# A gated residual in one VectorE pass, row means added back by ScalarE, and an order written out as a list

## The chip, the cores and the metric

The kernel runs on one core of a Trainium2 chip. A core has five engines that run their own instruction streams side by side: TensorE (PE in the profile, its weight loads PEld), VectorE (DVE), ScalarE (ACT), GpSimd (POOL) and SyncE (SP), whose stream here is little else than DMA issues. The metric is the device time of one launch in microseconds, smaller is better. Of the kernel before, three runs are shown: 843.17, 844.55 and 843.1 us, median 843.17.

## What is computed

The reference runs four sub-layers on a sequence of S = 2048 rows of D = 640 (all f32):

```
x = q
x = x + layernorm(x) * y            # A: gate
x = x + relu(layernorm(x) @ w1) @ w2  # B: MLP, Dff = 1728
x = x + layernorm(x) * y            # A again, same y
x = x + relu(layernorm(x) @ w1) @ w2  # B again, same weights
```

Here y is a long causal convolution (by FFT, over the sequence, for each channel) of kv = shortconv(k) * v with ssm_k, plus kv * ssm_D. It does not depend on x, so it is needed once. layernorm has no weights: (x − mean) / sqrt(var + eps) over a row of 640.

The fact that the change uses: layernorm does not see a constant added to a whole row. With r = 1/std and m the row mean, x + r(x − m)y = (x − m)(1 + r y) + m. If m is left out, the row that goes on differs from the reference's by a constant, which neither the next layernorm nor the matmuls behind it see. The constants have to be added back before the result is stored.

## The kernel before

**Tiling.** The 2048 rows are eight chunks of 256, each two row tiles of 128 x 640 (s = 0, 1). The convolution is done as matrix products on transposed data: `transform` turns kv and the filter into a short spectrum (tiles `pg`, `pt`, `pr`, with constant matrices `cG`, `cX`, `cM`), `products` multiplies spectra on VectorE (`pacc`, `pd`, `u`) and transforms back (`pq`, `qs`, then `yd` or `ys`). The finished y goes to a DRAM buffer `Y` and comes back by DMA as tile `y`, except for chunk 0 (the "direct" chunk), where `yd` is used straight from SBUF, and the last column blocks of some chunks, which are taken from `ys`.

**The MLP.** `prep` (L1115) does the gate and the second layernorm of one piece of a chunk, splits the result into two f16 parts (`xh`: high and low), transposes it to `xT`; `mm1` forms h as three f16 products of high and low parts (lines L1350, L1351, L1353; L1338 and L1340 for chunk 0), ScalarE and VectorE turn it into f16 `hh`, `hl` (L1493, L1494), `mm2` multiplies by w2 (L1322, L1323, L1325; tiles `o`, `oc`), and VectorE adds the scaled result to x (L1431). For the last chunks a scheme with fewer products is used (`wmm`, L1268). The weights are loaded as `ws` and scaled into f16 (`w`, L977).

**The gate.** `stats` (L1065) computes negm = −mean (ACT), the sum of squares (ACT, L1071), r (small ACT and DVE steps) and nmr = −r·mean, and then `xnA` = r·x + nmr on ACT (L1093). VectorE multiplies `xnA` by y (L1136, L1139 for the part from `ys`, L906 for chunk 0) and adds it to x with the row sum as a by-product for the next layernorm (L1143, L907 for chunk 0). Each is one instruction per row tile of 640 columns (chunk 0: pieces of 256, 256 and 128).

**Head and tail.** Before the first data arrive, PE runs matmuls on an identity that nobody reads (`spin`, L1602, and L1619 between the first real matmuls). VectorE adds `dDs` (ssm_D) to the first row of the filter tile `hf` (L538), and the matmuls `pg` of that tile follow. At the end the last pieces of `o` are added to x and stored (L1560, L1564, L1566; whole rows by L1437).

**What sets the order.** The program does not emit instructions directly: each step is handed to `Plan.op` with its engine, an assumed cost and the tiles that it reads and writes. A planner (`best`, `order`) then plays an event-driven schedule over these costs, with a rank for each step out of a table of numbers (`RANKS`), and emits the instructions of all engines in the resulting order. On the chip each engine runs its own stream in that order and waits on semaphores.

Of the kernel before, what the change touches and what calls it, by code (L numbers as in the profile page):

```python
# [22 lines left out]
P = 128  # L23
# [36 lines left out]
RANKS = (  # L60
    "D*!A2000311ONp91^@>D2mlEH3IGcL3;+!P4ge1T5C9PX5&#nb6aW<f762Cj7yuan8UPyr8~_~v9snNzAOIl%A^;-*BmgA<CIBY@C;$ThF90zBDF7`1E&wV3GypOHH2^jMIsiTZIRHHXK>$MlQUFu{"
    "Hvl^TLI6MjMgU*{R{&%HXaH;gZUA%uM*v6wNdQU!O8`s&O#n^+PXJH=SO8f7S^!%BTmW4FUI1SJJOF9{Q2==WeE@?1hX9iRqyUrvrU0t|umH9Iy8y!gFaS6JKLBq4MF3L(RsdoEWdLUYX#i~iaR7J#"
    "egJX+cL09?d;o#~ivWfIj{uecn*f~vq5ygTfB=O6i2#ZKkN}qepa7`=u>iRMp#Yo!W&s=l#Q@6y&j8Z^L;zI)VE}{xa{zS!hyaZMl>nLmp8$>kkpP$gr2wh`v;epOzW~Gl#{kIy%>btWtN^nBy#Txb"
    "zyQVo%mCH^+5qDK>HrV{E&)0L-vHzQ@BsAy^8k$jw*WH$B>^}AK>=9-VgXYDTLFs!YXOr1mI18+)dAZ9?f~=vN&#8{b^!$e3;`GcApwv9*8%7O>;d=z{Q>>~0s;pD+yM;&(E!x|*8toA-2mbM=m6^g"
    "@c{Aw_yBSNhXED=2mw_AkpcDq`T+d^0s#U5V*srHW&p1MYXGtUZ~(Ocb^y8ndjP=zfdI+?i~!OAk^tENnE>Dbo&e<lqX5tVr~udit^nQu?Evop`2hO>0RaR72LTTOz5wO`!T{+2$N>BR&H(-Z)Bpnk"
    "+W-;);Q$l?=Kvo8>;NYL_W&sY{{Sli3IQzv4goU(6#+Q`KmkYrPyto}TmfJKVF6_U009O82>}ZM4FMAY7XcmtZvh<vBLO4<ECCq-F#$9IHvu~VLIFkrOab!&O#xB?5dj(j8v!B#AOR);DgiP9F9AFO"
    "J^@7mO94><P61Z|WC3acXaQ^iZUJ)vh5>K^cL9O{dI5g{egT64hyjiPi~*7Xl>wRonE{>wp8=-<qXDS_ssXbBuK~FMxB<HXyaB=i!vV<w#{td(%>mN^(E;HBzyZVo<pKBtFab3IHUT{WL;*<wKLJAl"
    "SOHxDZ2@rsPXSZ`Ujb(UiUE%SV*zOabOC$;paG=;lmVy#t^uL}qyf4Cz5%fTv;npOtO2qC#sSa)$N|d%!2!hq$^py))B)cC;sNpj`~d+11p;*ecmaC>eF204i2;BCg#nxap#hfxn*q-O(gD~3<N>t-"
    "00P+o?E&=x`T-RJAOh(D69O0l`2h?9E&?+GECMtFKmr^BCjv17JOV}nNdiLxO#)K_TLMu6R{~!GWCC*ndIEj|umJ`F3IY)V83G*wA_6J`G6FUNI08KaK>|bqN&-#-R02{0S^{zcd;)(0ivo@Ulmd7H"
    "g#wKNk^+|kn*x;roC2f*s{*P5u>zq2rvj`3#R9eh!~($r%>vc}$O6>@&;rx~-vZ+T<^tLR-~#Fb1q1T}_X6nx?gI4!`~ndJ8v`E$CIdqQO9M{>w*i0xf&z#Fj{=hdnF6Q+uL8INxdOcczyiYp$pX&;"  # L70
    "*8<Z5+ybisy#ZbUfdRh(-2vVK-~rYF+5ztY?g8-u_5t((_W}O_0|E{L76JqU2?7rS3jz`X8Uh~zB?2S@D*`tHI|4oeNCI90EdpW!M*-&nc>(GHodFO6rU5kqMFLC$Y64IKSORVWbOM9|fdYpD`vC|7"
# [12 lines left out]
    "9|a}_F9kIPIt5MzS_N$dV+C*pN(7YzZv?gk&;-r|`vm<2vjn09w*<Qc!UV(w%>>{C<pk~oRRwPaSp{<idIf|9j0Keiodu!=hy|wwt_8RS#s$3v%>~j0)CJ20_66hwKn3&!Mg;=}3I#F+I0ZWeR|Rwh"
    "L<LI)dj(wuUIl&yg9U#DnFWCbrUkGCxdqAv&;`2%zy;3*+y&zW=mqNq>;(k|eFd5Y{sj&O7zQT>5(X0n83r5%9|j@@E(S6NHU>NfKn6_)Q3g{6Sq5JQU<P6aX9j8pZ3b}$a0Yb-c?Nw3e+GaC$OX;?"
    "(FN57+6CPO*#+JO<OSyi^9B3`<^}Hs0R{&K1O^HQ`2`jR9tI-@AO<D|5C$y<HwHBZItDQYK?XwxMg~;|M+Qy?TLxwZXa;TuRt8)Kb_RR~at3<_fd+&Ihz5)XiUyJfng*T*p$3lzmIjyxoCco;rUsn`"
    "qz0`9vj)8e!3M4dwg$=u+6L4H*apT1&IaHH?*``v@CM-q_67h4`343D{00RF3I`kqAO{Tx9S0-_D+ehDEe93{BL^=BF$XgTJqJbyNe4^^PX|s1QU_HBSqEGPI|g0`qXwl0s0OPBx(2)k#0JO)$p+O1"
    "%Lds7+XmbQ;|A&m0tW;K2nP%Y4hItl6bCQ|5(gUx83!^4IR{Y(R0miGUI%CgS_fhWZ3l1%cn5z6atDP6iwBVhp$Di3iU*Phtp~FQum`yZnFqZG#s|L##RtR(;|IwH%m>W}$_LU1=?Cox=LhZw*$3SR"
    "^9TF~{RadH2M8qyDhMtJJqSk#O9(&+L<mL*%?8s3U<Y9bX9sTwc?Wz4h6jlUj0cbhjt7$mng^Q)p9i7`rw6JBt_QaVwFkfly9dVyxCguk)(6f9$pr8OB?XuTwFSZj*9F@J^91Mw0tFHU7zG{$A_Xc1"
    "J_SPs>ILux_XYX|00ssI3<ePf7X}&z9R?}}F9taVJqA7oLIy|%Oa?y&YzBt~(*@rJjs@5Sp#{VR;sv|~?FHZk^#%9^<puo(@df_{0|p5O`vnaK6b2gxAqFJ|L<Ud>C<ZVFO9og5WCnN!g9e2Liv}YF"  # L90
    "E(Hh%6$U8=BnD3gQU*x{qy?%4tp&aX!3D<!%mv{E@&$7ScLsU}h6a%amj<8)u?DyXxdy5RuLipY-3ILj<_7f!{RROC)&?I30tQJ2S_TUSMFtNBD+XZ(GX`r0N(N~Leg<U*kOp)HjRuqkq6UHnn+B-{"
    "w+6ok#Rl;P{szYe(FXGd0|yBQ5eFp)9tS4}#RcvKjs}?qtOm3O%m&W}^aU&iGzK^ZR0dZDT?TIki3YF+7Y88+8V4c=E(bLSHwQZhKL<hwJO@DsMF(pKZU=D(bq9I}eFt3!l?Rgs-Uj6cl?K-arv}0X"
    ">ju6C^akGs`UVFF=>`i2_y!LL7zZW?{{|=rEC)0PItN1sbO(C}N(W5`cL#(Aj|Y|qqX(V`rUzpNhX(8hHU~!sKnG?AY6rCjvIf8g!v@d>(gxxN=mzoz_Xd;)oClZ(r3b4Au?MyXz6Zev$Oq5|*9Y7O"
    "@CWq=_Xqn200;vJ<p&-J5C>!jYzGwwUk54&J_mCLI0t?QX$OG^hX-~Cmj{9epa-c3uLp<+tOvRW%LmT~(+Bwn0SMIx-Ut2%1qciX6bKmz8VDQ+<Oc2rjR&#^!w13#-v{9b`vyb@NC!&?PzO^7R|i`M"
    "V+Vi-4+s?q5(pRwAqXc3F9<aVIS4xlEC@3QK?q3*RtQcAVF+djX9%4K<Ok>nqzCT@v<KP;^as%g{|D>`1_%lW_6H3J0tgWZ8wel>2?!$yDF`wMHwZ%rUI=OkN(fO1WC(Bwfe4HUk_eFql?Yb|X$V{h"
# [108 lines left out]
class Plan:  # L204
# [39 lines left out]
    def best(self):  # L244
        ranks = np.frombuffer(base64.b85decode(RANKS), "<u2").tolist()
        for o, r in zip(self.ops, ranks, strict=True):
            if o.prio[0] != CRIT:
                o.prio = (r, o.seq)
# [1499 lines left out]
```

## Time and profile before

| | |
|---|---|
| median of the runs shown | 843.17 us (843.1 to 844.55, 3 runs) |
| profiled execution, span | 841.6 us |
| PE busy | 833.6 us, 99% |
| DVE busy | 786.8 us, 93% |
| ACT busy | 522.8 us, 62% |
| DMA | 181.69 MB, mean 216 GB/s |
| chain that ended last | PE 79%, DVE 12%, DMA 3%, ACT 3%, issue 2% |

The profile is of one execution, whose span is from the first to the last instruction; the time of a run is taken on the device around it, and the runs shown lie 1.5 to 3.0 us above this span. A row such as `134.48 0.22 PE L1350 MATMUL h<-xT,w 128*128 128x128 f16 x1 [0.62 <-DVE hh L1494]` reads: start in us, duration in us, engine, line, operation, output and inputs, tile shape, count; in brackets how long the engine had been idle just before, and whose end it waited for. Durations overlap on PE, since the next matmul starts while the last one drains; how fast PE issues is read from the distance between starts. In a group's row, the numbers behind the bar are busy time in us, mean ns of one, and idle time ahead.

### The profile page before, as it was taken

The page shows a single profiled execution, that of the slowest core. Times are in us where ns is not written, and L with a number is a line of the kernel's source. Part 1 is how long each engine was busy: PE and PEld are TensorE (multiplying, and loading weights), DVE is VectorE, ACT ScalarE, POOL GpSimd, SP SyncE. Part 2 cuts the span into 40 slices and gives each one's busy share as a digit, 9 for nine tenths or more (in the row PEclk, how much of TensorE's full clock was granted, in tenths as well). Part 3 has the DMA queues.
Part 4 walks back from the last instruction along what each step waited for, and adds up shares of the span by engine and source line. Part 5 has one row for each costly group of instructions (what it writes and reads, how often), then busy time and mean ns, then how long its engine had stood idle before and what let it go on. Part 6 is the DMA issues. An engine that isn't in the chain of part 4 may idle for free.

```text
span 841.6 us, 20268 instructions
## 1 busy us (share of the span) xinstructions
PE 833.6 (99%) x8031; PEld 669.3 (80%) x8031; DVE 786.8 (93%) x1431; ACT 522.8 (62%) x1237; POOL 45.5 (5%) x56
## 2 busy tenths in 40 slices
PE   8999999999999999999999999999999999999998
PEld 7987887888888778777787777777777788888887
DVE  6999999999999999999999999999988799998775
ACT  5798887347776586647438574655524487868432
POOL 0000000000002111011110201010000000000000
PEclk9999999999999999999999999999999999999999
DMA  8995877987999997988998967688987466250400
GB/s 300 395 355 170 259 211 226 309 307 257 266 249 266 327 252 212 239 248 221 235 267 238 244 218 182 159 209 256 255 271 268 110 202 141 79 104 2 58 33 33
DMA packets 138145, 181.69 MB, mean 216 GB/s; under 512 B 53825, under 2 KB 95681, under 8 KB 138050
## 3 DMA queue, kind: packets, MB, share of 16 engines
q1 hardware_dynamic: 129586, 169.81, 67.4%
q0 software_dynamic: 8320, 10.49, 7.9%
q8 instruction: 63, 1.03, 0.5%
q14 instruction: 32, 0.26, 0.1%
q10 hardware_dynamic: 144, 0.10, 0.0%
HBM read 124.59 MB, written 34.08 MB: 189 GB/s over the span
## 4 chain that ended last, share of the span: by engine, by line
PE 79%; DVE 12%; DMA 3%; ACT 3%; issue 2%; SPq 0%; DVEq 0%; ACTq 0%
PE o L1268 10%; PE h L1350 8%; PE h L1351 8%; PE h L1353 8%; PE o L1323 7%; PE o L1322 7%; PE o L1325 6%; PE h L1338 4%; PE h L1383 2%; PE hs L1383 2%; PE h L1340 2%; PE oc L1322 2%; PE oc L1323 2%; PE oc L1325 2%; DVE pd L803 2%
## 5 line engine op out<-in xcount | busy, mean ns | idle before, releaser
L1350 PE MATMUL h<-xT,w 128*128 128x256 f16 (+1 forms) x1000 | 229.4, 249 | 0.9 <-DVE hh L1494 0.9
L1353 PE MATMUL h<-xT,w 128*128 128x256 f16 (+1 forms) x1000 | 229.2, 249 | 0.0
L1351 PE MATMUL h<-xT,w 128*128 128x256 f16 (+1 forms) x1000 | 229.2, 249 | 0.0
L1322 PE MATMUL o<-w,hh 128*128 128x512 f16 x336 | 127.3, 379 | 0.0
L1323 PE MATMUL o<-w,hh 128*128 128x512 f16 x336 | 127.3, 379 | 0.0
L808 DVE TENSOR_TENSOR pacc<-pacc,pd 128x1536 f32<-128x1536 f32 (+1 forms) x75 | 123.2, 1642 | 0.5
L1351 PEld LDWEIGHTS <-w 128*128 128x128 f16 x1100 | 107.6, 98 | 16.0 <-issue 1.8
L1350 PEld LDWEIGHTS <-w 128*128 128x128 f16 x1100 | 107.6, 98 | 14.5
L1353 PEld LDWEIGHTS <-w 128*128 128x128 f16 x1000 | 97.8, 98 | 6.3
L1493 ACT ACTIVATE hh<-h 128x512 f16<-128x512 f32 (+1 forms) x97 | 46.9, 485 | 69.1 <-PE h L1353 29.3
L1322 PEld LDWEIGHTS <-hh 128*128 128x128 f16 x672 | 65.7, 98 | 26.5
L1323 PEld LDWEIGHTS <-hh 128*128 128x128 f16 x672 | 65.8, 98 | 25.9
L803 DVE TENSOR_TENSOR pd<-Ax,Gx 128x768 f32<-128x768 f32 x83 | 78.3, 950 | 4.4 <-DMA Gx<-G 4.1
L1325 PE MATMUL o<-w,hl 128*128 128x512 f16 x208 | 78.8, 379 | 0.0
L1322 PE MATMUL oc<-w,hh 128*128 128x128 f16 x336 | 73.8, 220 | 0.0
L1323 PE MATMUL oc<-w,hh 128*128 128x128 f16 x336 | 73.6, 219 | 0.0
L532 ACT ACTIVATE tp<-kt,shs 128x256 f32<-128x256 f32 (+1 forms) x78 | 44.0, 577 | 26.8 <-DVE acc L606 20.8
L1325 PEld LDWEIGHTS <-hl 128*128 128x128 f16 x416 | 40.7, 98 | 24.5
L1338 PE MATMUL h<-xT,w 128*128 128x256 f16 (+1 forms) x400 | 57.9, 251 | 0.0
L1325 PE MATMUL oc<-w,hl 128*128 128x128 f16 x208 | 45.6, 219 | 0.0
L803 DVE TENSOR_TENSOR pd<-at,Gx 128x768 f32<-128x768 f32 x46 | 43.0, 950 | 0.7 <-DMA Gx<-G 0.5
L1338 PEld LDWEIGHTS <-w 128*128 128x128 f16 x400 | 35.9, 98 | 5.1
(284 smaller groups left out, 2010.3 us busy)
## 6 DMA issues: line engine op xcount, KB each, us to landing
Ax<-A SPq DMA_DIRECT2D x89, 384.0 KB, 4.2
Gx<-G SPq DMA_DIRECT2D x89, 384.0 KB, 4.4
A<-at SPq DMA_DIRECT2D x14, 768.0 KB, 6.3
G<-gt SPq DMA_DIRECT2D x14, 768.0 KB, 5.3
ws<-in_w SPq DMA_DIRECT2D x28, 320.0 KB, 6.8
y<-Y SPq DMA_DIRECT2D x22, 320.0 KB, 3.8
x<-in_q SPq DMA_DIRECT2D x16, 320.0 KB, 4.9
gs<-in_hF SPq DMA_DIRECT2D x20, 256.0 KB, 4.4
```

What stands on the lines that cost most here:

```text
L532: ACT.activation(o[:, i : i + m], kview(i, m, j), AF.Copy, scale=shs[:, t, j : j + 1])
L803: ew(f"mac{j % POOLMOD}", 768, lambda e, x=dst[i], av=av, gv=gv: e.tensor_mul(x.t, av(), gv()), [ax, gx], [dst[i]], pr_)
L808: dve(768 * (hi - lo), lambda lo=lo, hi=hi, pd=pd: DVE.tensor_add(acc[:, lo:hi], acc[:, lo:hi], pd[:, lo:hi]), [*sums[lo:hi], *dst[lo:hi]] ...
L1268: PE.matmul(b[:, c : c + w], x, y[:, z : z + w], start=done[i] == 1, stop=end, skip_group_check=fin)
L1322: PE.matmul(z, hh[:, c], wh[:, d], start=(j == JS[0] and i == 0 and (h == 0 or s == S[0])), stop=False)
L1323: PE.matmul(z, hh[:, c], wl[:, d], start=False, stop=end and tail)
L1325: PE.matmul(z, hl[:, c], wh[:, d], start=False, stop=end)
L1338: PE.matmul(p[:, z], wh, xv(t, x), start=b and x == 0, stop=e and x == 1)
L1350: PE.matmul(p[:, z], wh, xv(t, 0), start=b, stop=False)
L1351: PE.matmul(p[:, z], wh, xv(t, 1), start=False, stop=tail and e)
L1353: PE.matmul(p[:, z], wl, xv(t, 0), start=False, stop=e)
L1493: act(2 * R, lambda pv_=pv_, hh=hh: ACT.activation(hh.t, pv_(), AF.Relu), [src], [hh], URGENT)
```

## The change

**The gate.** `stats` for a gate no longer makes `nmr` and `xnA`; it returns r and negm. ACT makes t = r·y + 1 (two instructions where y comes in two parts), and VectorE does x = (x + negm)·t with the row sum in one instruction. So 44 multiplies leave VectorE's stream, and the 32 big `xnA` instructions of ACT become 44 for `t`. The row mean left out is kept: ACT writes it to `means` in the first gate, adds that of the second to it, and adds the sum to the row tile of x after the statistics of the second MLP (16 instructions of 128 x 640, L1109).

```diff
-            (0.19 * len(S), [r, negm], [nmr], lambda: [A(nmr[:, c], ...) for c in cols]),
+        if gated is not None:
+            a, layer = gated
+            if layer == 0:
...
+                act(2, lambda: ACT.activation(m[:, q_], negm[:, q_], AF.Copy, scale=-1.0), [negm], [m], FILL, 0.1)
+            else:
+                act(0, lambda: [ACT.activation(m[:, s : s + 1], negm[:, s : s + 1], AF.Identity, scale=-1.0, bias=m[:, s : s + 1]) for s in S], [negm, m], [m], FILL, 0.19 * len(S))
+            return r, negm
...
# prep, one row tile s
-            xns = stats(xs, sums, "A" + nm, S)
+            r, negm = stats(xs, sums, "A" + nm, S, gated=(a, layer))
-                ew("ay", cut, lambda e, s=s, xn=xns[s]: e.tensor_mul(xn[:, 0:cut], ys[s][:, 0:cut], xn[:, 0:cut]), ...)
+                gate_ = lambda o, i, s=s: ACT.activation(o, i, AF.Identity, scale=r[:, s : s + 1], bias=one.t)
+                act(cut, lambda s=s, t=t, gate_=gate_: gate_(t[:, 0:cut], ys[s][:, 0:cut]), [ys[s], r, one], [t], URGENT, 0.18)
-                dve(D, lambda ...: DVE.scalar_tensor_tensor(xs[s].t, xn.t, 1.0, xs[s].t, op0=ALU.mult, op1=ALU.add, accum_out=sums2[:, s : s + 1]), ...)
+                dve(D, lambda ...: DVE.scalar_tensor_tensor(xs[s].t, xs[s].t, negm[:, s : s + 1], t.t, op0=ALU.add, op1=ALU.mult, accum_out=sums2[:, s : s + 1]), ...)
...
+        for s in S if layer else ():
+            act(D, lambda s=s: ACT.activation(xs[s].t, xs[s].t, AF.Identity, bias=MEAN[a][:, s : s + 1]), [xs[s], MEAN[a]], [xs[s]], LATER, 0.1)
```

Chunk 0 gets the same two instructions for each of its pieces (L829, L830). A branch that sent the add through GpSimd and that no chunk took is dropped. In the weight norms, a matrix of ones becomes bf16 and four small matmuls read the upper half of their f32 operand.

**The order.** The planner and its ranks are gone; a table `ORDER` lists all steps in the order in which they are emitted:

```diff
-    def best(self):
-        ranks = np.frombuffer(base64.b85decode(RANKS), "<u2").tolist()
...
-        return self.order()
+    def table(self):
+        return [self.ops[k] for k in np.frombuffer(base64.b85decode(ORDER), "<u2")]
```

So the streams of all engines differ throughout, not at the gate alone. The start of SP's stream, which issues the first loads; before:

```order
L445 DMA cG<-in_cG 128x512
L515 DMA kt_0_157<-in_kT 128x262
L518 DMA hf_0_163<-in_hF 128x2x256
L439 DMA shs<-in_shk 128x20
L441 DMA dDs<-in_dD 1x640
L515 DMA kt_0_157<-in_kT 128x262
L518 DMA vt_0_186<-in_vT 128x2x256
L445 DMA cX<-in_cG 128x384
L518 DMA kt_2_202<-in_kT 128x2x262
L445 DMA cM<-in_cM 128x768
```

and after:

```order
L367 DMA cX<-in_cG 128x384
L440 DMA hf_0_176<-in_hF 128x2x256
L361 DMA shs<-in_shk 128x20
L367 DMA cG<-in_cG 128x512
L437 DMA kt_0_181<-in_kT 128x262 x2
L363 DMA dDs<-in_dD 1x640
L440 DMA vt_0_197<-in_vT 128x2x256
L440 DMA kt_2_203<-in_kT 128x2x262
L440 DMA vt_2_208<-in_vT 128x2x256
L440 DMA hf_2_210<-in_hF 128x2x256
L440 DMA hr_0_235<-in_hR 128x2x256
```

The first load is `cX` instead of `cG`, `dDs` is the seventh transfer or later instead of the fifth, and `cM` is no longer among these; it follows after two `x`, a `kt` and a `vt`. PE's stream has 38 spins ahead of the first `pg` before, and 21 after (56 in all in both); of the rest, four and eight stand between the pieces of the first `pg`, 23 between the first pieces of the second one. VectorE's stream begins with `hf + dDs` instead of an `acc` step.

VectorE's stream at the first piece of chunk 0's gate (`xnA` and `t` are the gate's tiles, `yd` the result of the convolution, `sp` the row sums, `u` and `park` the convolution's next pieces); before:

```order
L906 TENSOR_TENSOR xnA_00_462<-xnA_00_462,yd_432 128x256
L838 TENSOR_TENSOR u_2_486<-pacc_2_406 128x512
L907 SCALAR_TENSOR_TENSOR x_0_222,sp_0_96<-xnA_00_462,x_0_222 128x256
L906 TENSOR_TENSOR xnA_01_480<-xnA_01_480,yd_455 128x256
L824 TENSOR_TENSOR u_4_508<-park 128x256
L907 SCALAR_TENSOR_TENSOR x_1_241,sp_1_97<-xnA_01_480,x_1_241 128x256
```

and after:

```order
L760 TENSOR_TENSOR u_2_486<-pacc_2_449 128x512
L597 TENSOR_TENSOR gt_0_212<-gt_0_212 128x2x256
L830 SCALAR_TENSOR_TENSOR x_0_250,sp_0_99<-x_0_250,negmA_0_352,t_500 128x256
L874 SCALAR_TENSOR_TENSOR dg_530,ws_111<-pw_371,ident 128x128
L746 TENSOR_TENSOR u_4_541<-park 128x256
L830 SCALAR_TENSOR_TENSOR x_1_252,sp_1_100<-x_1_252,negmA_0_352,t_515 128x256
```

The two multiplies are gone, and a weight norm's step stands between the two row tiles.

The end of VectorE's stream (`o` is the result of the last matmuls, x_0 and x_1 the two row tiles of the last chunk); before:

```order
L1431 SCALAR_TENSOR_TENSOR x_1_10541<-o_12732,winv,x_1_10541 128x320
L1431 SCALAR_TENSOR_TENSOR x_1_10541<-o_12627,winv,x_1_10541 128x320
L1560 SCALAR_TENSOR_TENSOR x_0_10511<-o_12742,winv,x_0_10511 128x320
L1560 SCALAR_TENSOR_TENSOR x_0_10511<-o_12648,winv,x_0_10511 128x128
L1560 SCALAR_TENSOR_TENSOR x_0_10511<-o_12648,winv,x_0_10511 128x192
```

and after:

```order
L1371 SCALAR_TENSOR_TENSOR x_1_10527<-o_12685,winv,x_1_10527 128x320
L1500 SCALAR_TENSOR_TENSOR x_0_10508<-o_12704,winv,x_0_10508 128x320
L1500 SCALAR_TENSOR_TENSOR x_0_10508<-o_12699,winv,x_0_10508 128x128
L1371 SCALAR_TENSOR_TENSOR x_1_10527<-o_12597,winv,x_1_10527 128x320
```

The last step before was the last 192 columns of x_0, stored in a piece by itself; it is now half of x_1, and the store behind it takes all 640 columns of x_1.

More of the change, by code (lines that the diff above doesn't have):

```diff
@@ L357, in issue @@
+    def table(self):
+        return [self.ops[k] for k in np.frombuffer(base64.b85decode(ORDER), "<u2")]
     def issue(self):
-        out, end = self.best()
-        for o in out:
+        for o in self.table():
             for t in o.tiles:
@@ L364, in issue @@
             o.fn()
-        return end
 @with_exitstack
@@ L436, in tile_h3_mlp @@
     POOL.memset(c15.t, 1.5)
+    one = keep(const, [P, 1], "one")
+    POOL.memset(one.t, 1.0)
+    means = keep(const, [P, 2 * NC], "means")
     shs = keep(const, [P, NDT, 4], "shs")
@@ L1633, in early @@
         sums = load_x(a)
-        first[a] = (X[a], stats(X[a], sums, f"A{a}_0", both, URGENT, True), [keep(const, [P, 1, 3], f"sp{a}_{s}") for s in range(2)])
+        first[a] = (X[a], stats(X[a], sums, f"A{a}_0", both, URGENT, True, (a, 0)), [keep(const, [P, 1, 3], f"sp{a}_{s}") for s in range(2)])
     early(0)
```

304 lines of the change are left out of this document (118 added, 186 removed).

## The prediction

> **What bounds the kernel now.** I read the page's busy shares first, then its chain of waits, to see whether a VectorE saving can reach the end at all.
>
> ```profile
> PE 833.6 (99%) x8031; PEld 669.3 (80%) x8031; DVE 786.8 (93%) x1431; ACT 522.8 (62%) x1237; POOL 45.5 (5%) x56
> ...
> PE 79%; DVE 12%; DMA 3%; ACT 3%; issue 2%; SPq 0%; DVEq 0%; ACTq 0%
> ```
>
> VectorE (DVE), where the change saves work, is 93% busy, but TensorE (PE) is 99% busy and is 79% of the chain that ended last. These shares mix stages, so the second view is a table of windows; its columns are length, then busy time and count of PE, PEld, DVE, ACT, POOL, then granted clock, DMA share, GB/s.
>
> ```profile
> 0.00:20.00 20.00, 17.04 (x116) 14.97 (x117) 13.08 (x31) 11.25 (x25) 1.81 (x14) 1.00 0.87 296
> ...
> 80.00:140.00 60.00, 58.82 (x650) 48.63 (x649) 58.20 (x117) 47.18 (x123) 0.00 (x0) 1.00 0.72 227
> 235.00:630.00 395.00, 394.94 (x3379) 304.16 (x3377) 388.33 (x567) 229.46 (x542) 40.09 (x38) 1.00 0.89 240
> 630.00:841.56 211.56, 207.75 (x2102) 172.59 (x2101) 175.61 (x424) 124.42 (x294) 1.69 (x2) 1.00 0.40 103
> ```
>
> PE stands still in three places only: 20.00 − 17.04 = 2.96 us at the start, 60.00 − 58.82 = 1.18 us between 80 and 140 us, and 211.56 − 207.75 = 3.81 us in the last window, which is the tail. From 235 to 630 us it lacks 0.06 us. Is it busy with overlapped pipeline time, or really issuing as fast as it can?
>
> ```profile
> 300.89 0.27 PE L1351 MATMUL h<-xT,w 128*128 128x256 f16 x1
> 301.00 0.27 PE L1353 MATMUL h<-xT,w 128*128 128x256 f16 x1
> ```
>
> Starts are 0.11 us apart while one lasts 0.27: back to back. The matmuls are the same in number and shape after the change, so a VectorE saving is worth only what PE waits for VectorE. The view of PE's waits lists that (us in total, times, longest):
>
> ```profile
> PE h L1350 <- DVE hh L1494: 0.9, 2, 0.6
> PE pg L636 <- DVE hf L538: 0.8, 2, 0.4
> PE oc L1325 <- DVE hh L1494: 0.3, 1, 0.3
> ```
>
> The first and third rows are the 1.18 us between 80 and 140: three waits for `hh`. The timeline of the longest, on PE and on VectorE:
>
> ```profile
> 132.84 1.03 PE L659 MATMUL pg<-gs,cG 128*128 128x256 f32 x4
> 134.48 0.22 PE L1350 MATMUL h<-xT,w 128*128 128x128 f16 x1 [0.62 <-DVE hh L1494]
> ```
>
> ```profile
> 125.92 0.42 DVE L842 TENSOR_TENSOR u<-pacc 128x256 f32<-128x256 f32 x1 [1.19 <-DMA Y<-ys]
> 126.26 0.42 DVE L1494 SCALAR_TENSOR_TENSOR hh<-h,hh 128x256 f16<-128x256 f32 x1
> ...
> 132.81 1.28 DVE L1136 TENSOR_TENSOR xnA<-y,xnA 128x512 f32<-128x512 f32 x2
> 134.01 0.41 DVE L1494 SCALAR_TENSOR_TENSOR hh<-h,hh 128x256 f16<-128x256 f32 x1
> ```
>
> Two of the very multiplies that the change takes away (L1136) stand directly ahead of the `hh` that PE waits for. Four f32 matmuls from 132.84 are issued by 133.70 (four times the 0.216 us worked out below), so PE issued nothing for 0.78 us. The gap at 126 us (the shorter of the first row's two) is another thing: VectorE itself stood 1.19 us for a DMA ahead of that `hh`.
>
> **What the change costs and saves, engine by engine.** The groups concerned (busy us, mean ns of one, then idle before):
>
> ```profile
> L1093 ACT ACTIVATE xnA<-x,nmrA,rstdA 128x640 f32<-128x640 f32 x32 | 28.0, 910 | 0.1
> L1143 DVE SCALAR_TENSOR_TENSOR x<-xnA,x 128x640 f32<-128x640 f32 x30 | 24.4, 815 | 0.0
> L977 DVE SCALAR_TENSOR_TENSOR w<-ws,wsc,w 128x640 f16<-128x640 f32 x28 | 23.9, 878 | 0.3 <-ACT w L976 0.3
> L1136 DVE TENSOR_TENSOR xnA<-y,xnA 128x640 f32<-128x640 f32 (+2 forms) x30 | 22.4, 765 | 1.0 <-ACT xnA L1093 0.8
> L1104 ACT ACTIVATE jq<-x 128x640 f32<-128x640 f32 x16 | 11.7, 729 | 7.4 <-DMA x<-in_q 7.4
> L1139 DVE TENSOR_TENSOR xnA<-ys,xnA 128x128 f32<-128x128 f32 (+1 forms) x8 | 2.6, 347 | 0.0
> L906 DVE TENSOR_TENSOR xnA<-xnA,yd 128x256 f32<-128x256 f32 (+1 forms) x6 | 2.2, 368 | 0.0
> ```
>
> Removed from VectorE: 30 + 8 + 6 = 44 multiplies, 22.4 + 2.6 + 2.2 = 27.2 us busy. The 36 fused passes that stay (30 of L1143, 6 of L907) now take a per-partition scalar tile. No row has this exact form in f32; L977, the same operation with such a scalar, is 63 ns longer than L1143, so 36 x 0.063 = 2.3 us come back (bounds 0 and, if a pass cost as much as the two it replaces, 27.2). I take 2.3, the nearest row. That leaves 25 us.
>
> On ScalarE (ACT) the 32 L1093 become 44 of t = r*y + 1, the same operation with scale and bias, the cut pieces adding some ten fixed costs; 16 row-mean additions over 640 elements are new (0.73 us each as L1104, at most 0.91 as L1093: 11.7 to 14.6 us); the small ones nearly cancel (32 `nmr` go, 24 `means` come). About +12 to +20 us on an engine busy for 522.8 of 841.6. The mean additions touch an x that VectorE next adds to tens of us later, and that slack hides them; without it each would hold VectorE 0.73 us. I take 0 for them.
>
> Term 1, **the PE gaps**. The three gaps are 1.2 us in the wait view. Measured between starts, each is longer by the modelled end of the matmul before it (0.78 against 0.62 for the longest), so 1.2 + 3 x 0.16 = 1.7. With 25 us less on VectorE, most of it freed before PE's next need, I take all: −1.7. Bounds: 0 (the new order makes others) and −1.7, as PE has no other gap there.
>
> Term 2, **the head**. The new order also changes the first 20 us, before any gated residual.
>
> ```profile
> 1.95 4.24 PE L1602 MATMUL spin<-ident 128*128 128x128 f16 x38 [1.95 <-POOL heps L435]
> ...
> 10.14 0.72 PE L1619 MATMUL spin<-ident 128*128 128x128 f16 x10
> ...
> 14.36 2.42 PE L636 MATMUL pg<-hf,cG 128*128 128x256 f32 x10 [0.38 <-DVE hf L538]
> ...
> 18.35 0.81 PE L849 MATMUL pq<-u,cM 128*128 128x256 f32 x3
> ```
>
> ```profile
> 5.85 0.35 DVE L584 TENSOR_SCALAR acc<-kt,shs 128x256 f32<-128x256 f32 x1 [5.85 <-DMA shs<-in_shk]
> 6.12 0.41 DVE L538 TENSOR_TENSOR hf<-hf,dDs 1x256 f32<-1x256 f32 x1
> ```
>
> ```profile
> GB/s 0 0 0 0 0 158 222 343 346 133 167 221 236 301 208 254 283 230 229 290 243 206 249 261 288 282 349 307 307 338 407 397 402 376 393 363 395 375 373 360
> ...
> cM<-in_cM SPq DMA_DIRECT2D x1, 384.0 KB, 5.9
> ```
>
> (The last fence is the DMA view of 0 to 14 us.) The first real matmul follows the `hf + dDs` at 6.12; `cM` was issued 4.88 us in and landed 5.9 later, at 10.8. In the new order of SP's queue `dDs` is moved behind `cX` (192 KB) and a second `kt` (131 KB): 323 KB at the 250 to 300 GB/s of that stretch is 1.1 to 1.3 us. With VectorE's add now ahead of its `acc` step (0.27 us between the two starts) the first `pg` comes at about 7.5 instead of 6.6; if the tiny tile overtakes the large ones, no later than before. `cM` is moved behind `hr`, `vt`, `hf`, two `x`, `kt`, `vt`: 3 x 256 + 2 x 320 + 131 + 128 = 1667 KB, at the 380 GB/s after 10 us 4.5 us: it lands at 15.3. The PE list was rearranged to match: two thirds of `pg_2` and 23 spins now come ahead of `pr`, the first user of `cM`. At full rate PE gets there at about 16.2 (`hf_2`, with 2008 KB up to its end against 1880 for `cM` before, about 11.2, its add 0.4, then 2.7 us of `pg_2`, 0.4 of `pt_0`, 23 spins x 0.056 = 1.3), then `pr` 1.7, the rest of `pg_2` 0.9, `pt_2` 0.4: 19.2, where before the same set is done by 18.35. Head +0.9.
>
> The upper end comes from the PE rate. The 38 spins stand (4.24 − 0.27) / 37 = 0.107 us apart; the ten at 10.14 take (0.72 − 0.22) / 9 = 0.056; ten f32 of 256 columns 0.22 each. So PE ran at half rate for its first 4.0 us of work and at full rate ever after, though the window's clock column says 1.00. The new order has only 21 spins before the first `pg`: 2.2 us, ending near 4.2, then over 3 us of nothing. If it again takes 4.0 us of unbroken work, begun at 7.5, 2.0 us of that are lost: head +2.9. I take the middle, +1.9. The Trainium skill ("TensorE: Matmul & The Clock Gate", Part 1: The HAM clock gate) gives the mechanism: half rate until about one 3.4 us window of activity, on a free-running window; by it the head could be anything from 0.9 to about 2.6 (an estimate), and the trace agrees as far as 0.107 and 0.056 go.
>
> Term 3, **the tail**.
>
> ```profile
> 837.03 0.55 DVE L1560 SCALAR_TENSOR_TENSOR x<-o,winv,x 128x320 f32<-128x320 f32 x1 [0.33 <-PE o L1268]
> 837.86 0.68 DVE L1560 SCALAR_TENSOR_TENSOR x<-o,winv,x 128x128 f32<-128x128 f32 x2 [0.28 <-PE o L1268]
> ...
> 838.61 0.37 ACTq L1564 DMA_DIRECT2D out_dram<-x  x1
> ...
> DMA to landing us min/median/max: 2.2/2.2/2.2
> ```
>
> Before, the last two pieces are narrow and the last store is part of a row. After, the last step is 320 wide (0.55 instead of 0.68 for the two pieces: −0.13) and one store of all 640 columns follows, which lands 2.2 us after its issue (last row, the full-width store of L1437); the piece stored last before had from 838.61 to the end at 841.56, of which I allow 1.7 for landing. So +0.5 − 0.1 = +0.4 (bounds 0 and +0.7).
>
> Sum against the profiled execution: 841.56 + 1.9 − 1.7 + 0.4 = 842.2. The median of the runs shown, 843.17, lies 1.6 above this span, and I carry the same 1.6: **843.8 us**, +0.6, no change that a measurement can tell (0.2%, 1.7 us, is about what it can).
>
> **Rivals.** First, **faster**: `dDs` overtakes, PE is at full rate from the first `pg`, `pr` does not wait. For it: 2.5 KB against 256 KB tiles; 0.3 us earlier is possible, as the add no longer stands behind `acc`. Against it: 21 spins instead of 38, `cM` six places later. Head −0.3, gaps −1.7, tail 0: 839.6 + 1.6 = 841.2.
>
> Second, **slower**: the half rate lasts its whole 4.0 us after 7.5, and everything hung on `cM` arrives as late, so that only half of the gaps close. Head +2.9, gaps −0.8, tail +0.4: 844.1 + 1.6 = 845.7. It decides as soon as the `pg` after the first spins stand 0.43 apart for more than some 3 us; below that it is the forecast.
>
> Third, **the change does not do what its description says**. It speaks of fewer dependent neighbours; in the order of VectorE, 189 instructions now read a tile that the one right before wrote, against 95. What such a pair costs:
>
> ```profile
> 825.40 0.29 DVE L1394 TENSOR_TENSOR ha<-h,ha 128x128 f32<-128x128 f32 x1
> 825.73 0.42 DVE L1395 TENSOR_TENSOR ha<-hs,ha 128x256 f32<-128x256 f32 x1
> ...
> 828.41 0.28 DVE L1390 TENSOR_TENSOR ha<-h,ha 128x128 f32<-128x128 f32 x1
> 828.61 0.41 DVE L1431 SCALAR_TENSOR_TENSOR x<-o,winv,x 128x192 f32<-128x192 f32 x1
> ```
>
> Starts 0.33 apart when the next reads the result, 0.20 when it does not. 94 more pairs x 0.13 = 12 us, half of the 25 saved; if the other half also falls where VectorE waits anyway, the gaps stay: 841.56 + 1.9 + 0.4 + 1.6 = 845.5. Against it: VectorE still comes out 13 us ahead. The Trainium skill ("VectorE: DVE Perf Modes", The DRAIN you can't avoid) holds that a wait between neighbours costs nothing because each operation drains anyway. By it this rival would be empty; 0.33 against 0.20 says otherwise, and the measurement decides.
>
> **How the numbers follow.** Forecast 0.47 (its own range 842.0 to 844.8), faster rival 0.25, slow head 0.20, dependent neighbours 0.08. The first makes "same", the second "faster", the last two "slower": 0.25, 0.47, 0.28. The range takes in both signs: from 840.9, a little under the faster rival, to 846.2, a little over the slow head.
>
> **What would show it.** Gaps: PE's wait view loses its `hh` rows and 80 to 140 us is 60.0 busy. Head: the first `pg` at 7.5 rather than 6.6, its pitch 0.22 or 0.43, the first `pq` at 19 or later. Saving: DVE's busy time falls by about 25 us with its idle time growing as much, and ACT's rises by 12 to 20. Tail: the last matmul to the end takes 4.2 instead of 3.8. The forecast is wrong if PE's idle in 20 to 838 us grows, or if VectorE's 25 us buy PE time outside the three gaps, which I hold impossible at 0.11 us pitch.

## The result and the profile after

The changed kernel takes **855.29 us** (median of 4 runs, 853.16 to 855.63) against 843.86 us (843.1 to 844.96, 4 runs) for the kernel before beside it: a ratio of 1.013, 95% interval 1.0115 to 1.0145. It is 11.4 us slower. The prediction said 843.8 us, no difference, at most 846.2. It was wrong. In the experiments below, two single executions far longer than all others of their kernels, 2246.63 and 1237.2 us, are left out.

The page of the changed kernel, whose profiled execution has a span of 853.7 us (841.6 before):

```profile
PE 837.0 (98%) x8028; PEld 668.2 (78%) x8028; DVE 774.0 (91%) x1387; ACT 532.7 (62%) x1257; POOL 45.6 (5%) x57
...
PE 54%; DVE 21%; DMA 12%; ACT 7%; issue 4%; SPq 2%; POOLq 0%; DVEq 0%; ACTq 0%; POOL 0%
```

VectorE has less to do, as intended (774.0 against 786.8 us). Yet PE's share of the chain that ended last fell from 79% to 54%, and DMA's rose from 3% to 12%: the chain now leaves PE often, and through transfers. The windows of the changed kernel (length, then busy time and count of PE, PEld, DVE, ACT, POOL, then granted clock, DMA share, GB/s) say where:

```profile
0.00:20.00 20.00, 15.55 (x98) 13.28 (x99) 11.16 (x27) 7.30 (x15) 1.84 (x15) 1.00 0.88 284
20.00:80.00 60.00, 58.48 (x647) 50.55 (x646) 55.43 (x123) 52.52 (x115) 0.00 (x0) 1.00 0.80 270
80.00:140.00 60.00, 59.79 (x683) 48.82 (x682) 56.94 (x113) 46.90 (x123) 0.00 (x0) 1.00 0.76 243
...
235.00:630.00 395.00, 391.17 (x3358) 299.83 (x3356) 378.91 (x548) 235.65 (x557) 39.83 (x38) 1.00 0.90 240
...
760.00:853.60 93.60, 88.12 (x1051) 76.11 (x1049) 69.32 (x192) 45.04 (x102) 1.68 (x2) 0.99 0.21 43
```

The stretch at which the change was aimed did gain: PE's busy time in 80 to 140 us rose from 58.82 to 59.79 of 60. But from 235 to 630 us, where PE had lacked 0.06 us, it now lacks 395.00 − 391.17 = 3.83, and it lacks 1.52 between 20 and 80. PE's waits in the changed kernel (total us, times, longest):

```profile
PE h L1278 <- DMA xT<-xh: 4.6, 7, 1.3
PE pg L558 <- DVE hf L460: 2.5, 1, 2.5
...
PE h L1278 <- DMA xT<-xl: 1.5, 1, 1.5
PE oc L1265 <- DVE hh L1434: 0.8, 1, 0.8
PE o L1208 <- DVE gs L1429: 0.4, 1, 0.4
PE oc L1265 <- DVE hl L1434: 0.2, 1, 0.2
PE pq L771 <- ACT ob L585: 0.2, 1, 0.2
```

The first and third rows are new: eight waits, 6.1 us, in which the first product of a chunk (`mm1`) waits for the transposed activations `xT`. Before, PE waited for no `xT` at all. The transposes have not become slower. Of the transposes of `xT` (their tile's view), before:

```profile
DMA to landing us min/median/max: 2.5/3.9/8.1
```

and after, with the row of who waited:

```profile
  PE h L1278: 6.1, 8
...
DMA to landing us min/median/max: 2.6/3.5/8.2
```

They are issued later with respect to their use. Matching the issue and the landing of each transpose with the first matmul that reads its tile (36 tiles whose first use can be found in both traces), the last transpose of a tile is issued 7.3 us ahead of that matmul in the median before and 5.1 us after, and the last landing leads it by 3.7 us before and by 1.0 us after. What stands in that distance is seen at the second longest of these waits. The timeline of the changed kernel (start, duration, engine, line, operation):

```profile
750.82 0.91 ACT L1032 ACTIVATE xnB<-x,nmrB,rstdB 128x640 f32<-128x640 f32 x1
751.76 0.74 ACT L1113 ACTIVATE xh<-xnB 128x640 f16<-128x640 f32 x1
...
752.52 7.49 SPq L1141 DMA_TRANSPOSE xT<-xh  x4
...
753.62 0.90 ACT L1032 ACTIVATE xnB<-x,nmrB,rstdB 128x640 f32<-128x640 f32 x1
754.91 0.72 ACT L1113 ACTIVATE xh<-xnB 128x640 f16<-128x640 f32 x1
756.65 0.82 DVE L1114 TENSOR_TENSOR xh<-xnB,xh 128x640 f16<-128x640 f32 x1
...
761.18 0.30 PE L1208 MATMUL o<-w,hl 128*128 128x320 f16 x1
762.83 0.28 PE L1278 MATMUL h<-xT,w 128*128 128x256 f16 x1 [1.34 <-DMA xT<-xh]
```

The first row tile is normalised at 750.82, the second only at 753.62, with weight scaling between them on ScalarE, and its low part on VectorE (L1114) comes at 756.65, behind other steps. SP issues the four transposes over 7.49 us, the last at 758.7 us. That one lands at 762.8, and PE has stood still since 761.5. It carries the high part of the second row tile, which was ready at 755.6 (754.91 + 0.72); SP's list has it behind the transpose of the low part, so it waited for VectorE too.

The other part of the loss is the head. PE's timeline of the changed kernel:

```profile
1.95 2.42 PE L1542 MATMUL spin<-ident 128*128 128x128 f16 x21 [1.95 <-POOL heps L354]
6.87 3.78 PE L558 MATMUL pg<-hf,cG 128*128 128x256 f32 x8 [2.50 <-DVE hf L460]
...
12.31 0.59 PE L558 MATMUL pg<-hf,cG 128*128 128x256 f32 x2
...
18.04 1.89 PE L620 MATMUL pr<-sh,cM 128*128 128x256 f32 x8
...
21.07 1.06 PE L558 MATMUL pg<-hf,cG 128*128 128x128 f32 x8
```

The first `pg` come at 6.87, 0.43 us apart until about 11.9 and 0.22 after that. The work that was done by 18.35 us before is done by 21.07: 2.7 us, in this execution.

The new gate itself costs what its rows of before said (groups of the changed kernel: busy us, mean ns of one):

```profile
L1081 DVE SCALAR_TENSOR_TENSOR x<-x,negmA,t 128x640 f32<-128x640 f32 x30 | 25.9, 879 | 0.6 <-ACT t L1076 0.2
L1076 ACT ACTIVATE t<-y,one,rstdA 128x640 f32<-128x640 f32 (+2 forms) x30 | 25.2, 866 | 0.0
...
L1109 ACT ACTIVATE x<-x,means 128x640 f32<-128x640 f32 x16 | 13.1, 822 | 0.0
```

The fused pass takes 879 ns, 64 more than the old addition (815); 63 was predicted.

### The profile page after: what moved, and what is told of

It reads as the page before. It is cut to its first block, busy times and chain, and to the rows that moved or that the text cites. A ratio compares the mean times of both kernels' runs of the same rounds, so it can differ in the third digit from the quotient of the medians.

```text
span 853.7 us, 20236 instructions
## 1 busy us (share of the span) xinstructions
PE 837.0 (98%) x8028; PEld 668.2 (78%) x8028; DVE 774.0 (91%) x1387; ACT 532.7 (62%) x1257; POOL 45.6 (5%) x57
## 4 chain that ended last, share of the span: by engine, by line
PE 54%; DVE 21%; DMA 12%; ACT 7%; issue 4%; SPq 2%; POOLq 0%; DVEq 0%; ACTq 0%; POOL 0%
PE o L1208 5%; PE h L1290 5%; PE h L1293 5%; PE h L1291 5%; PE o L1262 4%; PE o L1263 4%; PE o L1265 4%; DVE pacc L730 3%; DVE pd L725 3%; DMA Gx<-G 3%; PE h L1278 3%; DMA xT<-xh 3%; PE pg L558 2%; PE h L1323 2%; PE hs L1323 2%
```

## The experiments

The change has two parts, a gate and an order, and a theory for each: that the gate costs (a new wait, the mean additions), or that the order does.

**The gate in the old order.** Every old step keeps its old place, `t` stands where the multiply stood, and the mean additions halfway between their inputs and the first user of their result. VectorE's stream against that of before, at one gate:

```diff
 TENSOR_TENSOR gt_2<-gt_2 128x2x256
-TENSOR_TENSOR xnA_1_00<-y_1_00,xnA_1_00 128x640
 TENSOR_TENSOR acc_4<-acc_4,tp_4 128x256
-SCALAR_TENSOR_TENSOR x_0,sums_1_0<-xnA_1_00,x_0 128x640
+SCALAR_TENSOR_TENSOR x_0,sums_1_0<-x_0,negmA_1_0,t_1_00 128x640
```

> The new gate (t on ScalarE, one VectorE pass, row means put back) with the order of the kernel before: every step that exists in both stands where it stood, t stands where the multiply stood. Theory 'order' (the 12 us come from the new order alone): no PE wait for xT, first pq near 18.4 us, the gaps for hh smaller; 841.5 us, at most 844. Theory 'gate' (t in series behind y on ScalarE makes the second layernorm and so the transposes late): PE waits for xT of 4 us and more, 849 or more.

Measured: 844.97 us (10 runs), 1.0016 of before (1.0007 to 1.0026). The wait for `xT` is gone, and so are some 10 of the 11.4 us: **the order costs, not the gate**. But the gate gains nothing either, and the window and the waits of this kernel show that PE stands still in the stretch of the old gaps for as long as before, if for other steps:

```profile
80.00:140.00 60.00, 58.77 (x650) 48.53 (x649) 55.05 (x110) 47.89 (x126) 0.00 (x0) 1.00 0.73 229
```

```profile
PE oc L1262 <- DVE x L1525: 0.8, 1, 0.8
...
DVE x L1081 <- ACT t L1076: 3.6, 4, 1.5
```

The first row is PE's longest wait behind the head. VectorE's busy time in 80 to 140 fell from 58.20 to 55.05 us, and PE's is as it was (58.82, now 58.77). VectorE now waits for ScalarE's `t`, 1.5 us at the longest.

**The old gate in the new order**, the complement: `xnA` stands where `t` stood, and the multiply right ahead of the addition.

```diff
-SCALAR_TENSOR_TENSOR x_0,sp_0<-x_0,negmA_0,t 128x256
+TENSOR_TENSOR xnA_00<-xnA_00,yd 128x256
+TENSOR_TENSOR xnA_01<-xnA_01,yd 128x256
+SCALAR_TENSOR_TENSOR x_0,sp_0<-xnA_00,x_0 128x256
```

> The old gate with the new order: xnA stands where t stood, the multiply where the fused pass stood, just ahead of the add. Theory 'order': at least as slow as the change, 854 to 860 us, since the late transposes stay and VectorE has 25 us more to do. Theory 'gate': head loss only, 846 us.

Measured: 889.33 us, 1.0535 (1.0508 to 1.0561). That is far above what either theory gave. It is no clean price of the gate, because the serial place makes a wait of its own:

```profile
DVE xnA L1055 <- ACT xnA L1012: 14.4, 11, 2.4
```

It shows only that the new order has no room for the old gate.

**The head alone.** The new order with its first 147 steps in the old sequence:

```diff
 L1542 MATMUL spin<-ident_81 128x128
-L558 MATMUL pg_0_189<-hf_0_176,cG 128x2x128 x4
...
+L1542 MATMUL spin<-ident_81 128x128
+L558 MATMUL pg_0_216<-hf_0_166,cG 128x2x128 x4
```

> The changed kernel, but its first 147 steps in the old order (loads, 38 spins in one row, first spectra), all behind them in the new order. If the 2.7 us by which the first pq is later go straight through to the end: 852.5 us. If they are taken up by the later PE waits for xT: 855, as the change.

Measured: 853.75 us, 1.011 (1.0091 to 1.013). So of the 2.7 us by which the head is late about 1.5 reach the end, with intervals that overlap. The rest of the loss stays. The waits of PE, from the profile of the fastest of the four runs (850.82 us), have 4.4 us for `xT`:

```profile
PE h L1278 <- DMA xT<-xh: 2.9, 5, 0.9
...
PE h L1278 <- DMA xT<-xl: 1.5, 1, 1.5
```

**The half rate in the head**, on the kernel before: 21 instead of 38 spins ahead of the first `pg`, nothing else.

```diff
-        pe(..., lambda: PE.matmul(spin[:, 0:P], ident16.t, ident16.t, ...), [ident16], [spin], IDLE)
+        pe(..., lambda k=k: PE.matmul(spin[:, 0:P], ident16.t, ident16.t, ...) if k < 21 else None, [ident16], [spin], IDLE)
```

> The kernel before with 17 of its 38 first spins left out (they compute nothing that is read): loads and all else stay, the first pg at 6.6 us as before. If PE's rate at the start hangs on those spins: pg 0.43 apart for 3 to 4 us, the first pq 1.5 to 2 us later, 845.3 us. If not: pitch 0.22 and 843.6.

Measured: 845.9 us, 1.0023 (1.0012 to 1.0034). PE's timeline of this kernel:

```profile
1.95 2.42 PE L1602 MATMUL spin<-ident 128*128 128x128 f16 x21 [1.95 <-POOL heps L435]
6.40 4.64 PE L636 MATMUL pg<-hf,cG 128*128 128x256 f32 x10 [2.03 <-DVE hf L538]
...
14.76 1.99 PE L698 MATMUL pr<-sh,cM 128*128 128x256 f32 x8 [0.24 <-ACT sh L693]
```

The ten `pg` stand 0.43 us apart, and `pr` starts at 14.76 instead of 11.99: 2.8 us late, without any change of the loads. So the missing spins alone make a head as late as the changed kernel's, and about 2 us of it show in the time (1.0 to 2.9 by the interval).

**Is it VectorE's load?** In the new order, every third of the long `pacc` additions is left out, 21 in all.

```diff
-dve(768 * (hi - lo), lambda ...: DVE.tensor_add(acc[:, lo:hi], acc[:, lo:hi], pd[:, lo:hi]), ...)
+dve(768 * (hi - lo), lambda ...: None if skip else DVE.tensor_add(acc[:, lo:hi], acc[:, lo:hi], pd[:, lo:hi]), ...)
```

> The changed kernel without every third of VectorE's long additions pacc += pd of the convolution (some 25 of 1.64 us, 40 us of VectorE; y is then wrong). Theory 'in the new order VectorE has no room left': the waits for xT and hh go, 846 to 848 us, the head's 2.7 us stay. Theory 'it is ScalarE's or SP's queue': 853 or more.

Measured: 852.66 us, 1.0112 (1.0097 to 1.0127), with VectorE at 740.6 us, 33.4 less. That is 2.6 us faster than the changed kernel, with intervals that overlap. The waits for `xT` stay as long (6.1 us, as in the changed kernel):

```profile
PE h L1280 <- DMA xT<-xh: 4.4, 5, 1.6
...
PE h L1280 <- DMA xT<-xl: 1.7, 1, 1.7
```

The lateness of the transposes does not come from VectorE's load. Since the same steps in the old order have no such wait, what is left is where the steps stand.

**What the waits for `xT` are worth.** `mm1` reads a weight tile in the place of `xT`, in the new order and, as a control, in the kernel before; the transposes still run.

```diff
-        xv = lambda t, x: xt[x][:, t, x0 : x0 + R]
+        xv = lambda t, x, j: WT[j, 0, 0][:, x, 0:R]
```

> The changed kernel with the first MLP product reading weights in place of xT (the product is then wrong, its matmuls the same in number and shape): PE no longer waits for any transpose, all else stands where it stood. Theory 'what is lost behind the head is lost where PE waits for xT': 6 us of waits and what follows from them go, 847 to 849 us. Theory 'PE would only wait for the next late thing (hh, hl)': 853 or more.

> The same edit in the kernel before, which shows no PE wait for xT: 843.6 us by both theories, within 1 us; more than 2 us less would say that the edit itself saves time, and the reading of the other run would fall.

Measured: 849.12 us in the new order, 1.0053 (1.0033 to 1.0073), and 843.25 us before, 0.9995 (0.9986 to 1.0004). The edit changes nothing where PE did not wait for `xT`, and takes 6.2 us off where it did: just the 6.1 of the wait rows. **By these medians more than half of the loss is this one hand-off.** With the same edit and the old head besides:

> The changed kernel with the old head and without waits for xT, both edits together. If head and transposes are the whole loss: 844 to 846 us. If some third thing holds more than 2 us: 848 or more.

Measured: 847.3 us, 1.0046 (1.003 to 1.0062). Some 4 us are left over the control, between what the two theories gave. Its waits of PE show small hand-offs of another kind:

```profile
PE oc L1265 <- DVE hh L1434: 1.6, 2, 0.9
...
PE oc L1265 <- DVE hl L1434: 0.5, 1, 0.5
```

**Can the hand-off be mended by moving it up?** Three attempts in the new order. First the whole preparation of a chunk up to 16 places earlier on its engines, a piece of VectorE's stream:

```diff
+RECIPROCAL stdA_0<-stdA_0 128x2
 TENSOR_TENSOR sd_4<-acc_4 128x128
...
 TENSOR_TENSOR at_0<-at_0 128x2x256
-RECIPROCAL stdA_0<-stdA_0 128x2
```

> The changed kernel with the steps of each piece's preparation (y load, gate, statistics, xnB, xh, transposes) each moved up to 16 places earlier in the list, some 3 to 4 us, as far as their inputs allow. Theory 'order, too little lead': PE's waits for xT fall from 6.1 us to under 1.5 and the time to 849 or 850. Rival 'the chain to xh or the DMA queues are too slow wherever the steps stand': within 1 us of 855.

Measured: 959.36 us, 1.137 (1.1352 to 1.1388), which neither theory had. Then `xnB`, `xh` and the transposes 10 places earlier, here a piece of ScalarE's stream and one of SP's:

```diff
+ACTIVATE xnB_0_01<-x_1,nmrB_0_0,rstdB_0_0 128x640
 ACTIVATE hh_6<-h_6 128x128
 ACTIVATE x_1<-x_1,means 128x640
-ACTIVATE xnB_0_01<-x_1,nmrB_0_0,rstdB_0_0 128x640
...
+DMA_TRANSPOSE xT_0_10<-xh_0_11 128x5x128
 DMA hr_2<-in_hR 128x2x256
```

> The changed kernel with only xnB, xh and the transposes moved up to 10 places earlier in the list (the statistics, the gate and the y loads stay). Theory 'these steps stand too late': xT waits fall from 6.1 us to under 2, 850 us. Theory 'moving steps up in queues that run in order blocks what stands behind them, as when the whole preparation was moved': 860 or more.

Measured: 895.86 us, 1.062 (1.0605 to 1.0636). And each half of that move alone: the rows of ScalarE above with those of `xh` on VectorE, or the rows of SP above:

> The changed kernel with xnB and xh (ScalarE and VectorE) up to 10 places earlier, the transposes where they were. If the loss of the run that moved all three came from VectorE and ScalarE standing for each other: 880 us or more. If it came from SP's queue: 850 to 856.

> The changed kernel with the transposes alone up to 10 places earlier in the list, so that they stand in SP's queue ahead of loads that they were behind. If SP stands at them until xh is there and holds the loads up: 865 us or more and longer waits of VectorE for Gx. If SP had room: 850 to 856, with fewer waits for xT.

Measured, two runs each: 873.92 us, 1.0363 (1.0338 to 1.0387), and 875.69 us, 1.0384 (1.0364 to 1.0404). Against the changed kernel each half costs about 20 us and both together 41. What a step does that stands ahead of its input is shown by VectorE's waits with the whole preparation moved,

```profile
DVE stdA L1000 <- ACT stdA L998: 31.9, 11, 8.8
```

by VectorE's with `xh` moved,

```profile
DVE xh L1114 <- ACT xh L1113: 19.2, 8, 7.2
```

and by SP's with the transposes moved:

```profile
SPq L1141 <- ACT xh L1113: 46.6, 5, 26.7
```

The moved step waits at the head of its engine's stream, and everything behind it waits too; SP stands up to 26.7 us for one transpose, with the convolution's loads behind it. Moving these steps up while all others keep their places does not mend the hand-off. That an order without the wait exists is shown by the old one.

**Why does the gate gain nothing in the old order?** First, `t` 8 places earlier on ScalarE:

```diff
+ACTIVATE t_1_00<-y_1_00,one,rstdA_1_0 128x640
 ACTIVATE tp_4<-kt_4,shs 128x256
-ACTIVATE t_1_00<-y_1_00,one,rstdA_1_0 128x640
```

> The new gate in the order before, with each t moved up to 8 places earlier, so that VectorE does not stand for t. Theory 'the freed VectorE time went into waits for t': VectorE's wait for t falls from 3.6 us to under 1, the gaps between 80 and 150 us shrink, 843.0 us. Rival 'ScalarE then stands for y': 845.5 or more.

Measured: 844.6 us, 1.0015 (1.0005 to 1.0025), as without the move, though VectorE's wait for `t` (L1081) fell from 3.6 us to 1.0. So that wait was not what ate the gain. Second, the mean additions left out:

```diff
-            act(D, lambda s=s: ACT.activation(xs[s].t, xs[s].t, AF.Identity, bias=MEAN[a][:, s : s + 1]), ...)
+            act(D, lambda s=s: None, ...)
```

> The new gate in the old order without the sixteen additions of the row mean (the output then lacks the means). If those 13 us of ScalarE are what eats the gain: 843.0 us or less, against 844.97 with them. If it is t, which VectorE now waits for: 844.5 to 845.2, no change.

Measured: 842.59 us, 0.9996 (0.9987 to 1.0005), and the stretch is nearly full:

```profile
80.00:140.00 60.00, 59.85 (x663) 49.23 (x662) 56.42 (x111) 47.93 (x127) 0.00 (x0) 1.00 0.74 235
```

So the 16 mean additions cost 1.0016 − 0.9996, some 1.7 us, and they are what made the other gaps: PE is busy for 59.85 us of 60 without them, 58.77 with them. Can they be placed for nothing? On GpSimd, and right behind their inputs on ScalarE:

```diff
-            act(D, lambda s=s: ACT.activation(xs[s].t, xs[s].t, AF.Identity, bias=MEAN[a][:, s : s + 1]), ...)
+            gps(D, lambda s=s: POOL.tensor_scalar(xs[s].t, xs[s].t, MEAN[a][:, s : s + 1], None, op0=ALU.add), ...)
```

> The new gate in the old order, the sixteen row mean additions on GpSimd in place of ScalarE. If they only cost by standing in ScalarE's queue: 842.6 to 843.2, as the run without them. If x comes too late from GpSimd, or VectorE is slowed by it: 845 or more.

```diff
 ACTIVATE xnB_1_00<-x_0,nmrB_1_0,rstdB_1_0 128x640
+ACTIVATE x_0<-x_0,means 128x640
 ACTIVATE xh_1_00<-xnB_1_00 128x640
```

> The new gate in the old order, each row mean addition on ScalarE directly behind the last step that it depends on, some 20 to 35 us earlier than in the run with 844.97. If ScalarE's time as such is the price, or it delays the hh or xh behind it there: 844.5 to 846. If the place was bad: 843.

Measured: 845.91 us, 1.0026 (1.0012 to 1.004), and 848.21 us, 1.0059 (1.0039 to 1.008). Neither is better than halfway on ScalarE, and the second lies above what was expected of it. On GpSimd one addition takes 2.39 us, and VectorE's busy time rises from 767.5 to 774.1 us though it has the same instructions.

```profile
L1109 POOL TENSOR_SCALAR x<-x,means 128x640 f32<-128x640 f32 x16 | 36.7, 2394 | 260.4 <-ACT xnB L1032 260.4
```

**Are the old gaps worth anything?** In the kernel before, the three `hh` passes that PE waited for are moved ahead of their neighbours on VectorE, one, one and two places:

```diff
+SCALAR_TENSOR_TENSOR hh_1<-h_1,hh_1 128x256
 TENSOR_TENSOR xnA_0_00<-y_0_00,xnA_0_00 128x512
 TENSOR_TENSOR xnA_0_01<-y_0_01,xnA_0_01 128x512
-SCALAR_TENSOR_TENSOR hh_1<-h_1,hh_1 128x256
```

> The kernel before with three steps of its VectorE stream moved: the three hh for which PE waits at 94, 126 and 133 us stand one, one and two places earlier. If these gaps are lost time, as the prediction took them: all 1.7 us come back, 841.9 us. If PE only waits elsewhere instead: 843.6.

Measured: 843.7 us, 0.9997 (0.9988 to 1.0006). The three waits are gone, and PE's waits of this kernel name others:

```profile
PE h L1269 <- DVE hh L1435: 0.7, 2, 0.5
...
PE pr L617 <- DVE gt L584: 0.4, 1, 0.4
```

Closing the gaps of the forecast was worth nothing measurable, since the next hand-off on VectorE is late in their place.

## Why the prediction was wrong, by its steps

**What bounds the kernel** was right: PE, issuing back to back. Its own reading of 235 to 630 us, 0.06 us of idle time in 395, had a consequence that was not drawn: there a new order could bring nothing but loss.

**The VectorE saving** was over-estimated: 25 us predicted, 19.3 measured with the gate alone (767.5 against 786.8) and 12.8 with the new order (774.0). The 25 summed the durations of rows, and such durations overlap: in a row that the prediction shows, a step of 0.28 us is followed by the next after 0.20. The two orders have the same VectorE instructions. If the 90 or so more dependent neighbours of the new order account for their difference of 6.5 us, one costs 0.07 us; the rival on them took 0.13. They decided little in any case: taking five times as much off VectorE bought 2.6 us, and even that is not clear of the noise. The sentence of the Trainium skill that was weighed there ("VectorE: DVE Perf Modes", The DRAIN you can't avoid), that a wait between neighbours costs nothing extra, is not settled by this: no run tells the neighbours from whatever else differs between the two orders.

**ScalarE** was to gain 12 to 20 us; it gained 9.9 (532.7 against 522.8). **The mean additions**, taken at 0, cost some 1.7 us, measured in the old order. The slack to their user is there, but they stand in ScalarE's stream ahead of steps that VectorE and PE wait for; which one was not singled out.

**Term 1, the PE gaps (−1.7)**, is the step that failed. "With 25 us less on VectorE [...] I take all" is false by the experiment without the mean additions and by the one that moved `hh`: the gaps close, and the kernel is as fast as before (1.1 us faster at the most, by the end of the first one's interval). Worse were the bounds, "0 (the new order makes others) and −1.7". The sentence names the danger and prices it at no more than the gain. A whole order was replaced, and I compared the streams at the head, at the gate and at the end only. The distance from a transpose to its first reader, 7.3 us before, could have been followed in SP's, ScalarE's and VectorE's streams for each chunk; it fell to 5.1, with 3.5 us of that for landing. That hand-off alone costs 6.2 us, by the run without it. None of the rivals had this mechanism, and the rival of the third kind, that the change does not do what its description says, looked at neighbours and not at hand-offs.

**Term 2, the head (+1.9, bounds 0.9 and 2.9)**, was right in mechanism, and in the profiled execution near its upper bound: 2.7. The first `pg` came at 6.87, not 7.5, as `dDs` did not arrive that late. The half rate then lasted 5.0 us (6.87 to 11.9) and cost 2.5, not 2.0. `cM` landed 4.2 us after its issue at 10.83, at 15.0 (predicted 15.3), and was not waited for. The parts of its 16.2 us at full rate add up to 16.0, so the lower bound should have been 0.7. Where between the bounds the head comes out is partly luck, since the half rate does not last equally long in every execution of the same head. In the kernel with the whole preparation moved up it ended earlier:

```profile
6.82 3.43 PE L558 MATMUL pg<-hf,cG 128*128 128x256 f32 x8 [2.45 <-DVE hf L460]
10.09 0.39 PE L1542 MATMUL spin<-ident 128*128 128x128 f16 x4
10.31 0.65 PE L558 MATMUL pg<-hf,cG 128*128 128x256 f32 x2
```

The four spins from 10.09 stand 0.055 us apart there, and 0.107 in the changed kernel (from 10.44). About 1.5 us of the head reached the end, by runs whose intervals overlap.

**Term 3, the tail (+0.4)**, was right. From the end of the last matmul to the end of the span it takes 853.7 − 849.5 = 4.2 us, as predicted:

```profile
849.17 0.30 PE L1208 MATMUL o<-w,hl 128*128 128x320 f16 x1
...
850.50 0.39 SPq L1377 DMA_DIRECT2D out_dram<-x  x1
```

**The sum.** As PE bounds the kernel, what is lost must show as time in which PE starts nothing, or starts at half rate. The two profiled executions differ by 853.7 − 841.6 = 12.1 us. The head is 2.7 and the tail 0.4. The eight waits for `xT` are 6.1; measured between starts each is 0.16 longer, as in Term 1, which makes 7.4. The other four waits behind the head in that view (`hh`, `gs`, `hl`, `ob`) are 1.6, or 2.2 between starts, against the 1.7 of the gaps before: 0.5 more. That is 11.0 of 12.1; the other 1.1 was not traced. The mean additions' 1.7 is no further term: it was measured in the old order, and what they cost in the new one must lie inside these waits, where no run took them out. By the runs, `xT` is 6.2 and the head about 1.5 of the 11.4, and the kernel without both still lies some 4 us above the control, of which no run singles out the parts.

Of the prediction's own signs, the one for its being wrong came true: PE's idle between 20 and 838 us grew. The sign for the gaps nearly came true as well (80 to 140 us busy for 59.79 of 60, and one `hh` row left, in another stretch), and was worth nothing.

## What to carry to other kernels

When the engine that bounds a kernel runs back to back, a new order can only lose there, so price it hand-off by hand-off: for each transfer or converted tile that this engine reads, the distance from its last producer step to the first reader, before and after, against what the producer takes to land. Work saved on another engine is worth no more than the waits it ends, less those that come up behind them. And a late step is not mended by moving it ahead of its own input: on engines that work in order it then holds up everything behind it; 19 to 104 us were lost here by moves that were to win back some 6.

## What the runs showed of the hardware

The half rate at the start is not one fixed stretch of work. It took in all 4.0 us of unbroken spins in the kernel before, 5.0 us of work after a pause in the changed kernel, and about 5.9 us, after a pause too, in the kernel with 21 spins, while the clock column showed 1.00 in all of them. Nor does a given head fix it: with 38 unbroken spins it lasted 3.1 us in the profiled execution with the mean additions on GpSimd and 5.1 in the one with `t` moved up; with 21 spins and a pause it lasted 2.9 us from the first `pg` in the one with the whole preparation moved up, against the 5.0. The Trainium skill ("TensorE: Matmul & The Clock Gate", Part 1: The HAM clock gate) has about 3.4 us with a free-running window; the measured stretches lie on both sides of that, and their spread over executions of the same head fits that the window does not start with the work.

GpSimd takes 2.39 us for an addition that ScalarE makes in 0.82, and with 16 of them there VectorE's busy time was 6.6 us longer with the same instructions. The longer ones are VectorE steps that run beside such an addition: the `gt` step (L597) at 217.6 us took 1.76 us, where the median of its row is 0.69.
